# Batch 1's first Fourier step moved into the first items, with the data as stationary operand

## The chip, the cores and the metric

The kernel runs on 1 core of one Trainium2 chip. The metric is the device time of one execution in microseconds (us), the median of several runs. TensorE (PE) multiplies matrices; PEld is its weight load; VectorE (DVE), ScalarE (ACT) and GpSimd (POOL) work beside it; SyncE (SP) issues most transfers, in order, and waits at a transfer that may not start yet. Each engine executes its instructions in the order in which they are written.

## The reference

```python
# x: (2, 3008, 256); then an MLP pair on the 6016 rows
X = np.fft.rfft(x, axis=1)
Yr = Xr @ w_r - Xi @ w_i + b_r
Yi = Xr @ w_i + Xi @ w_r + b_i
Yr = np.sign(Yr) * np.maximum(np.abs(Yr) - 0.01, 0.0)     # Yi the same
y = np.fft.irfft(Y, n=3008, axis=1)
h = y @ w_in;  g = np.maximum(h, 0) + alpha * np.minimum(h, 0);  x = g @ w_out
h = x @ w_in2; g = np.where(h >= 1, h, np.where(h <= -1, 0, (h + 1) ** 2 / 4)); return g @ w_out2
```

## The kernel before

The length 3008 is split as 47 x 64. A forward transform is two matmul steps: the **first step** over the 47 (`f1`), the **second step** over the 64 with the twiddle factors (`f2_parts`). Rows of `x` come in 16 groups `g`, 8 for each batch. `f1(g)` has the 96 x 96 matrix of cosines and sines as stationary operand and 4 x 256 columns of x as moving operand; ACT and DVE copy the result from PSUM to a tile `ae`. The second step needs other rows on a partition, so `store_a` writes `ae` to HBM (`a_dr`), in two halves, and `load_a` reads it back as `a_sb[b]`, in parts. All of this is issued on SP in program order, between loads of `x`, `c_f2` (tiles `m`) and `c_i1` (tiles `n`). All 16 groups of `f1` stand ahead of the first item.

Then come 24 **items** (b, i), 12 for each batch, in a loop over `j`. In pass j TensorE executes, in this order: the second step of item j+2 (`psf`, 4 matmuls), a mixing sum of item j+1 (`psk`), two mixing products of item j (`ri`), the inverse transform's first step of item j-2 (`psi`); in passes 16 to 21 also one `p3` (`ps`, 32 matmuls of 64 x 64 tiles), the inverse transform's last step for batch 0. ACT and DVE split `psf` into a high and a low part (`fh`, `fl`) and a sum `s`, add the bias (`ri<-psk,b_t`), shrink, and copy `psi` (`ve`) and `ps` (`yt`). Between the items the weights of the MLP are converted (`conv`). After the loop the MLP begins (`first`: `psh`), a dense run of matmuls to the end.

An fp32 matmul is two instructions in the profile, so 32 matmuls are x64 there.

PSUM has 8 banks. Six belong to tags of one or two buffers in the pool `psum` (`e` has two; `o0` to `o3`, `ri` and `psk` among them, one each); tag `h` has two. A tile that takes a buffer over waits until the last tile in it has been read.

Of the kernel before, what the change touches and what calls it, by code (L numbers as in the profile page):

```python
# [18 lines left out]
NK = 24  # L19
# [12 lines left out]
def fourier_constants():  # L32

    import numpy as np

    n1, k1 = np.arange(R1), np.arange(NK)
    a = 2 * np.pi * (np.outer(n1, k1) % R1) / R1

    c = np.zeros((2, 48, 2, 2, NK))
    for par in range(2):  # L40
        c[par, :R1, 0, par] = np.cos(a)
        c[par, :R1, 1, par] = -np.sin(a)
    c = c.reshape(96, 4, 2, NK // 2).transpose(0, 2, 1, 3).reshape(96, 96)

    g = np.zeros((2, 64, 64))
# [26 lines left out]
    return (c.astype(f), m.reshape(128, NK * 128).astype(f),  # L72
            w.reshape(128, NK * 128).astype(f), g.astype(f))
# [21 lines left out]
def spectral_mlp_kernel(ctx: ExitStack, tc: tile.TileContext, x, w_r, w_i, bias, c_f1, c_f2,  # L95
                        c_i1, c_i2, w_in1, w_out1, alpha, w_in2, w_out2, out):
# [5 lines left out]
    psum = ctx.enter_context(tc.tile_pool(name="psum", bufs=2, space=PSUM))  # L102
    dram = ctx.enter_context(tc.tile_pool(name="dram", bufs=1, space=DRAM))
# [29 lines left out]
    a_dr = [[dram.tile([NT, 48, D], F32, name=f"a_dr{b}_{h}") for h in range(2)] for b in range(B)]  # L133
# [214 lines left out]

    c47 = block("u2", [128, 1024], F32, "c47")[0:96, 0:96]
    A.dma_start(c47, c_f1)  # L350
    xs = {}

    def load_x(g):
        b, j = divmod(g, 8)
        tag = f"p{g}" if g < 6 else f"w{g - 6}" if g < 14 else f"c{g - 12}"
        xs[g] = block(tag, [96, 4, D], F32, f"x{b}_{j}")
        if g == 0:
            nc.sync.dma_start(xs[g][:, 0:1, :], x[b, j, :, 0:1, :])
            nc.sync.dma_start(xs[g][:, 1:4, :], x[b, j, :, 1:4, :])
        else:  # L360
            nc.sync.dma_start(xs[g], x[b, j])
# [3 lines left out]
    def load_a(b, parts):  # L365
        if a_sb[b] is None:
            a_sb[b] = block(f"a{b}", [128, NK, D], F32, f"a_{b}")
        for k, n in parts:
            h, k0 = divmod(k, NK // 2)
            src = a_dr[b][h].rearrange("t (q k) f -> (t q) k f", q=4)  # L370
            nc.sync.dma_start(a_sb[b][:, k:k + n, :], src[:, k0:k0 + n, :])

    def store_a(g, h):
        b, j = divmod(g, 8)
        nc.sync.dma_start(a_dr[b][h][4 * j:4 * j + 4].rearrange("t p f -> p t f"), aes[g][48 * h:48 * h + 48])
# [7 lines left out]
    a_sb, aes = [None] * B, {}  # L383

    def f1(g):
        b, j = divmod(g, 8)
        if g < 10:
            ae = block(f"w{8 + g}" if g < 5 else f"m{1 + g}" if g < 8 else f"w{g - 8}", [96, 4, D], F32, f"ae{g}")
        else:
            if g == 10:  # L390
                late.append(block("a1", [96, 6, 4, D], F32, "ae_late"))
            ae = late[0][:, g - 10]
        aes[g] = ae
        for i in range(2):
            ps = psum.tile([96, 2, D], F32, tag="h" if i else "e", name=f"ps1_{b}_{j}_{i}")
            for u in range(2):
                T.matmul(ps[:, u, :], c47, xs[g][:, 2 * i + u, :], start=True, stop=True)
# [5 lines left out]
    late = []  # L403
# [5 lines left out]
    slopes = base.tile([128, 128], F32, name="slopes")  # L409
    alpha_t, sign, slope, flips = (slopes[:, NF * k:NF * k + NF] for k in range(4))  # L410
    flips = flips.bitcast(U32)
    A.dma_start(alpha_t, alpha)
# [4 lines left out]
    V.memset(ones, 1.0)  # L417
    for g in range(8):
        f1(g)
        store_a(g, 0)  # L420
        load_x(8 + g)
        if g == 3:
            load_mn(0, m_t, c_f2, 0)
        if g in (1, 2):
            A.dma_start(wm32[g - 1], (w_r, w_i)[g - 1].rearrange("(c p) e -> p c e", p=128))
    load_a(0, A_PARTS[:2])
    load_mn(0, m_t, c_f2, 1)
    load_a(0, A_PARTS[2:5])
    load_mn(1, m_t, c_f2, 0)
    load_mn(0, n_t, c_i1, 0)  # L430
    for g in range(8):
        store_a(g, 1)
    load_mn(1, m_t, c_f2, 1)
    load_mn(0, n_t, c_i1, 1)
    load_a(0, A_PARTS[5:])
# [3 lines left out]
    next(conv)  # L439
# [3 lines left out]
    def f2_parts(b, i, **where):  # L443

        ps = psum.tile([128, 2, 2, 2, R2], F32, **(where or {"tag": "h"}), name=f"psf{b}_{i}")
        for k in range(2):
            for c in range(2):
                T.matmul(ps[:, :, c, k, :], a_sb[b][:, 2 * i + k, c * 128:(c + 1) * 128],
                         m_t[i // 4][:, (2 * i + k) % 8, :], start=True, stop=True)
        return lambda: parts_of(b, i, ps)  # L450

    def parts_of(b, i, ps):
# [3 lines left out]
        ps = ps.rearrange("p t c k n -> p (t c k n)")  # L456
        t = rot.tile([128, 512], F32, tag="ta" if (b, i) < (0, 2) else "tb", name=f"s32_{b}_{i}")
        xi, s32 = t[:, 0:256], t[:, 256:512]
        xt[b, i] = tuple(v.rearrange("p (t c n) -> p t c n", t=3, c=2) for v in (xh, xl))

        def op(name):
            if name == "i":
                A.activation(xi, ps[:, 256:512], AF.Copy)
            elif name == "s":
                V.tensor_tensor(s32, ps[:, 0:256], xi, op=ALU.add)
            elif name == "H":
                A.activation(xh[:, 0:512], ps, AF.Copy)
            elif name == "L":
                V.tensor_tensor(xl[:, 0:512], ps, xh[:, 0:512].bitcast(F32), op=ALU.subtract)
            elif name == "h":  # L470
                A.activation(xh[:, 512:768], s32, AF.Copy)
            elif name == "l":
                V.tensor_tensor(xl[:, 512:768], s32, xh[:, 512:768].bitcast(F32), op=ALU.subtract)
# [14 lines left out]

    wm = [block(t, [128, 2, 2, D], F32R, f"wm{k}") for k, t in enumerate(("c0", "c1", "w2"))]
    ws = [rot.tile([128, 2, D], F32, tag=t, name=f"ws{t}") for t in ("cm", "cp")]  # L490

    def split_wm(k, w):
        hi, lo = (wm[k][:, z].rearrange("p c (h q) -> p c q h", h=2) for z in range(2))
        split(w.rearrange("p c (q h) -> p c q h", h=2), hi, lo, A)

    for g in range(8, 16):
        f1(g)
        if g < 15:
            store_a(g, 0)
        if g == 8:  # L500
            T.matmul(ri[0].rearrange("p z e -> p (z e)"), ones, b_t[0:1].rearrange("p z e -> p (z e)"), start=True, stop=True)
            V.tensor_copy(b_t, ri[0])
        if g == 9:
            split_wm(0, wm32[0])
            V.scalar_tensor_tensor(ws[0], wm32[0], -1.0, wm32[1], op0=ALU.mult, op1=ALU.subtract)
        if g == 11:
            split_wm(1, ws[0])
            V.tensor_tensor(ws[1], wm32[1], wm32[0], op=ALU.subtract)
        if g == 13:
            split_wm(2, ws[1])  # L510
# [118 lines left out]
    def first(l, c, f, before):  # L629
        n = chunks[c][2]  # L630
        xh, xl = xc[l, c]
        tag = "e" if f % 2 and (c > 4 or c < 2 and f < 4 - 2 * c) else "h"
        ps = psum.tile([128, NMAX], F32, tag=tag, name=f"psh{l}_{c}_{f}")[:, :n]
# [36 lines left out]
    ops = [f2_parts(*items[0], tag="o3", bufs=1), f2_parts(*items[1], tag="e"), None]  # L670
    ops[:2] = [v() for v in ops[:2]]
    for what in "0i 0s 0h 1i 0l 0H 1s 0L 1h k0 1l 1H f2 r0 1L 2i".split():
# [6 lines left out]
        else:  # L679
            ops[int(what[0])](what[1])  # L680
    for name in "HshLl":
        ops[2](name)
    store_a(15, 0)
    for j in range(n):
        parts = f2_parts(*items[j + 2]) if 0 < j < n - 2 else None
        if j + 1 < n:
            mix_sum(*items[j + 1])
        if parts is not None:
# [5 lines left out]
        if j == 3:  # L694
            for g in range(8, 16):
                store_a(g, 1)
        if j == 5:
            load_a(1, A_PARTS[:2])
        if j == 6:
            load_mn(2, n_t, c_i1, 0)  # L700
            load_a(1, A_PARTS[2:3])
            load_mn(2, n_t, c_i1, 1)
            load_a(1, A_PARTS[3:5])
        if j == 9:
            load_a(1, A_PARTS[5:])
# [19 lines left out]
    prep(0, 1)  # L725
    first(0, 0, 0, None)
# [174 lines left out]
    def quad(p, j, prev, extra, last=False):  # L901
# [5 lines left out]
        def product_of(op):  # L907
            if op in ("M1", "M5"):
                k = "AC"[op == "M5"]
                ps[k] = psum.tile([128, NMAX], F32, tag="h", name=f"ps{k}{l}_{p}_{j}")[:, :m]  # L910
# [177 lines left out]
```

## Time and profile before

| | |
|---|---|
| median of 3 runs | 1102.14 us (1100.82 to 1102.43) |
| profiled execution | 1102.65 us, of which its span 1100.6 us |
| PE busy | 1087.2 us (99%) |
| DVE, ACT, POOL busy | 897.4, 815.9, 36.9 us |
| DMA | 101.19 MB, mean 92 GB/s |

The span is the time from the first to the last instruction. A busy share is that of an engine over the whole span; the kernel has stages, so what a change of one stage is worth is read from the rows of that stage. A row of the timeline merges neighbours that are alike; its bracket says how long the engine was idle before it and what ended that.

### The profile page before, as it was taken

The page shows a single profiled execution, that of the slowest core. Times are in us where ns is not written, and L with a number is a line of the kernel's source. Part 1 is how long each engine was busy: PE and PEld are TensorE (multiplying, and loading weights), DVE is VectorE, ACT ScalarE, POOL GpSimd, SP SyncE. Part 2 cuts the span into 40 slices and gives each one's busy share as a digit, 9 for nine tenths or more (in the row PEclk, how much of TensorE's full clock was granted, in tenths as well). Part 3 has the DMA queues.
Part 4 walks back from the last instruction along what each step waited for, and adds up shares of the span by engine and source line. Part 5 has one row for each costly group of instructions (what it writes and reads, how often), then busy time and mean ns, then how long its engine had stood idle before and what let it go on. Part 6 is the DMA issues. An engine that isn't in the chain of part 4 may idle for free.

```text
span 1100.6 us, 17043 instructions
## 1 busy us (share of the span) xinstructions
PE 1087.2 (99%) x6368; PEld 955.7 (87%) x6368; DVE 897.4 (82%) x1572; ACT 815.9 (74%) x1499; POOL 36.9 (3%) x36
## 2 busy tenths in 40 slices
PE   9989999999999999999999999999999999999998
PEld 6878888888888998888889988888899888888897
DVE  3769759888879979989999877877878878878876
ACT  3557776656776768888888777877778878777876
POOL 0025400000000000000000000000000000000000
PEclk9999999999999999999999999999999999999999
DMA  9898754101322403324226720010010000100101
GB/s 265 299 277 261 204 142 108 39 1 67 126 97 97 171 20 115 115 96 141 89 97 248 273 90 1 1 39 1 1 38 1 37 1 1 39 1 1 39 1 37
DMA packets 49860, 101.19 MB, mean 92 GB/s; under 512 B 5009, under 2 KB 27249, under 8 KB 49778
## 3 DMA queue, kind: packets, MB, share of 16 engines
q1 hardware_dynamic: 48832, 99.41, 27.6%
q8 instruction: 50, 0.82, 0.3%
q10 hardware_dynamic: 946, 0.69, 0.2%
q14 instruction: 32, 0.26, 0.1%
HBM read 64.57 MB, written 35.52 MB: 91 GB/s over the span
## 4 chain that ended last, share of the span: by engine, by line
PE 82%; ACT 3%; DVE 2%; issue 0%; ACTq 0%; DVEq 0%
PE pq L114 10%; PE pq L115 10%; PE pq L116 10%; PE seeded L114 4%; PE seeded L116 4%; PE seeded L115 4%; PE psh L114 4%; PE pso L114 4%; PE psh L116 4%; PE psh L115 4%; PE pso L116 4%; PE pso L115 4%; PE psA L114 3%; PE psA L116 3%; PE psA L115 3%; PE psC L116 3%
## 5 line engine op out<-in xcount | busy, mean ns | idle before, releaser
L114 PE MATMUL pq<-gh,w 128*128 128x512 f32 (+1 forms) x576 | 216.6, 376 | 1.0 <-ACT yt L874 1.0
L115 PE MATMUL pq<-gl,w 128*128 128x512 f32 (+1 forms) x576 | 216.0, 375 | 0.4 <-DVE gl L845 0.2
L116 PE MATMUL pq<-gh,w 128*128 128x512 f32 (+1 forms) x576 | 215.8, 375 | 0.0
L842 ACT ACTIVATE gh<-ta 128x512 fp32r<-128x512 f32 (+1 forms) x144 | 88.0, 619 | 92.1 <-DVE ta L839 85.9
L641 ACT ACTIVATE ta<-psh,slopes 128x512 f32<-128x512 f32 (+1 forms) x96 | 65.1, 678 | 78.7 <-DVE ta L643 42.3
L114 PEld LDWEIGHTS pq<-gh,w 128*128 128x128 f32 x576 | 108.8, 189 | 15.9 <-ACT yt L874 3.1
L115 PEld LDWEIGHTS pq<-gl,w 128*128 128x128 f32 x576 | 108.9, 189 | 13.7 <-DVE gl L845 1.0
L116 PEld LDWEIGHTS pq<-gh,w 128*128 128x128 f32 x576 | 108.9, 189 | 12.8
L845 DVE TENSOR_TENSOR gl<-tb,gh 128x512 fp32r<-128x512 f32 (+1 forms) x96 | 65.3, 680 | 60.8 <-ACT gh L842 60.7
L845 DVE TENSOR_TENSOR gl<-ta,gh 128x512 fp32r<-128x512 f32 (+1 forms) x144 | 97.3, 676 | 3.1 <-ACT gh L842 1.4
L111 DVE TENSOR_TENSOR gl<-ta,gh 128x512 fp32r<-128x512 f32 (+1 forms) x96 | 65.2, 679 | 37.9 <-ACT gh L108 37.5
L933 DVE TENSOR_TENSOR h<-psC,s 128x512 f32<-128x512 f32 (+1 forms) x72 | 48.8, 678 | 40.8 <-PE psC L116 34.1
L114 PE MATMUL psh<-mxh,w 128*128 128x512 f32 (+1 forms) x192 | 72.2, 376 | 0.1
L114 PE MATMUL pso<-gh,w 128*128 128x512 f32 (+1 forms) x192 | 72.3, 377 | 0.0
L116 PE MATMUL pso<-gh,w 128*128 128x512 f32 (+1 forms) x192 | 71.9, 375 | 0.0
L115 PE MATMUL psh<-mxl,w 128*128 128x512 f32 (+1 forms) x192 | 71.9, 375 | 0.0
L116 PE MATMUL psh<-mxh,w 128*128 128x512 f32 (+1 forms) x192 | 71.9, 375 | 0.0
L115 PE MATMUL pso<-gl,w 128*128 128x512 f32 (+1 forms) x192 | 71.9, 375 | 0.0
L643 DVE SCALAR_TENSOR_TENSOR ta<-psh,slopes,ta 128x512 f32<-128x512 f32 (+1 forms) x96 | 70.5, 734 | 0.0
L839 DVE SCALAR_TENSOR_TENSOR tb<-tb,h 128x512 f32<-128x512 f32 (+1 forms) x96 | 60.7, 673 | 0.0
L831 ACT ACTIVATE ta<-ta 128x512 f32<-128x512 f32 (+1 forms) x96 | 59.3, 617 | 1.6
L842 ACT ACTIVATE gh<-tb 128x512 fp32r<-128x512 f32 (+1 forms) x96 | 59.3, 618 | 0.0
(163 smaller groups left out, 2640.1 us busy)
## 6 DMA issues: line engine op xcount, KB each, us to landing
s<-kept SPq DMA_DIRECT2D x32, 512.0 KB, 4.3
u<-in_w_in SPq DMA_DIRECT2D x32, 256.0 KB, 3.0
u<-in_w_out SPq DMA_DIRECT2D x32, 256.0 KB, 3.3
kept<-sh SPq DMA_DIRECT2D x16, 512.0 KB, 2.9
kept<-wh SPq DMA_DIRECT2D x16, 512.0 KB, 2.7
w<-kept SPq DMA_DIRECT2D x16, 512.0 KB, 5.5
v_dr<-ve SPq DMA_DIRECT2D x12, 512.0 KB, 3.9
v<-v_dr SPq DMA_DIRECT2D x32, 192.0 KB, 5.3
```

The source lines that it names most:

```text
L111: V.tensor_tensor(lo, src, hi.bitcast(F32), op=ALU.subtract)
L114: T.matmul(ps, wl, xh, start=start, stop=False, skip_group_check=chained)
L115: T.matmul(ps, wh, xl, start=False, stop=False, skip_group_check=chained)
L116: T.matmul(ps, wh, xh, start=False, stop=stop, skip_group_check=chained)
L641: A.activation(ta, ps, AF.Copy, scale=slope[:, f:f + 1])
L643: V.scalar_tensor_tensor(ta, ps, sign[:, f:f + 1], ta, op0=ALU.mult, op1=ALU.max)
L831: A.activation(self.t, self.t, AF.Square)
L839: V.scalar_tensor_tensor(self.t, self.t, 1.0, self.h, op0=ALU.min, op1=ALU.max)
L842: A.activation(halves(self.gh, self.m), like_halves(self.t, self.m), AF.Copy)
L845: V.tensor_tensor(halves(self.gl, self.m), like_halves(self.t, self.m), halves(self.gh, self.m).bitcast(F32), op=ALU.subtract)
L933: V.tensor_tensor(blk.h, ps[x], ps[y_], op=ALU.add)
```

## The change

Batch 0 keeps its first step, its stores and its loads. For batch 1 `f1` is replaced by `f1_points(g)`: x is the stationary operand, 64 of its columns at a time on 64 (or 48) partitions, and 48 columns of cosines and sines (`c_p1`, held in `slopes[:, 64:128]`) are the moving operand. Its 32 matmuls for a group go to four 64 x 64 tiles of the array. The result has the layout that the second step wants, so two copies put it into `a_sb[1]`, and nothing goes to HBM. Groups 8 and 9 stand ahead of the first item, groups 10 to 15 in passes 0 to 5, between `psk` and `ri`. The second step of batch 1 is now 8 matmuls of 64 rows for an item, with its own constants (`c_p2`, tiles `mp`, 6 loads of 512 KB); its result takes two banks, so tag `h` becomes a pool of its own that holds two buffers of one bank, then, from pass 10 to the end of the loop, one buffer of two banks. The inverse step's `psi` moves to tag `e` from pass 10 on. Loads of batch 1's x move behind the first loads of `a_0`, and the splits of the mixing weights (`split_wm`) and the bias matmul move into and behind batch 0's `f1`.

```diff
-    for g in range(8, 16):
-        f1(g)
-        if g < 15:
-            store_a(g, 0)
...
+    def f1_points(g, second=V):
+
+        v = xs[g].rearrange("p (q d n) -> p q d n", q=2, d=8)
+        ps = [psum.tile([128, 8, 2 * NK], F32, tag="e", name=f"ps1_1_{g}_{r}") for r in range(2)]
+        for d in range(8):
+            for q in range(2):
+                for r, rows in enumerate((slice(0, 64), slice(64, 112))):
+                    T.matmul(ps[r][64 * q:64 * q + 64, d, :], v[rows, q, d, :], g47[rows, 0:48], start=True, stop=True)
+
+        def evict():
+            for r in range(2):
+                d0 = 16 * (g - 8) + 8 * r
+                dst, src = a_sb[1][:, :, d0:d0 + 8], ps[r].rearrange("p d k -> p k d")
+                if r and second is V:
+                    V.tensor_copy(dst, src)
+                else:
+                    A.activation(dst, src, AF.Copy)
...
+            ps = htile([128, 2, 2, 2, 2, R2], name)[:, :, 0]
+            for k in range(2):
+                n = 2 * i + k
+                for z in range(2):
+                    for c in range(2):
+                        rows = slice(64 * c, 64 * c + 64)
+                        T.matmul(ps[:, c, :, k, :], a_sb[1][rows, 2 * n + z, :], mp_t[n // 4][rows, n % 4, z, :],
+                                 start=z == 0, stop=z == 1)
...
-        ps = [psum.tile([128, D], F32, tag="h", name=f"psi{b}_{i}_0"),
+        ps = [htile([128, D], name) if (b, i) < (0, 8) else psum.tile([128, D], F32, tag="e", name=name),
...
+    f1_points(8)()
+    late = f1_points(9)
...
     for j in range(n):
+        if j == 10:
+            h_pool(1)
         parts = f2_parts(*items[j + 2]) if 0 < j < n - 2 else None
         if j + 1 < n:
             mix_sum(*items[j + 1])
+        if j < 6:
+            late = f1_points(10 + j, A)
...
-        if j == 3:
-            for g in range(8, 16):
-                store_a(g, 1)
-        if j == 5:
-            load_a(1, A_PARTS[:2])
+        if j < 6:
+            late()
+        if j in (5, 7, 8, 9, 11, 12):
+            load_mp((5, 7, 8, 9, 11, 12).index(j))
```

The order of instructions changes at three places that matter below. The first is TensorE in pass 0, around the mixing products of item 0. Before:

```order
L486 MATMUL psk_1_379<-wm_239,fl_1_342 128x256 [waits DVE_49]
L486 MATMUL psk_1_379<-wm_239,fl_1_342 128x256
L486 MATMUL ri_77<-wm_240,fh_0_338 128x256 x4
L486 MATMUL ri_77<-wm_240,fl_0_339 128x256 x2
L486 MATMUL ri_77<-wm_241,fh_0_338 128x256 x4
```

After (`ps_1_10` is group 10 of the first step; 30 more of its matmuls follow where the dots are):

```order
L566 MATMUL psk_1_384<-wm_128,fl_1_346 128x256 [waits DVE_49]
L566 MATMUL psk_1_384<-wm_128,fl_1_346 128x256
L440 MATMUL ps_1_10_0_392<-slopes,x_105 64x48 [waits DVE_49,DMAHW6_49,PE_49,Pool_49]
L440 MATMUL ps_1_10_1_393<-slopes,x_105 64x48 [waits DVE_49]
...
L566 MATMUL ri_75<-wm_129,fh_0_337 128x256 x4
```

Group 10 now stands ahead of the products, and its second matmul waits for DVE: its buffer of tag `e` is that of `psk_1`, which DVE reads in `ri_76<-psk_1`. On DVE that instruction now has a copy more ahead of it, four rows up:

```order
L549 TENSOR_TENSOR fl_1_346<-psf_1_340,fh_1_345 128x512 [waits Activation_49]
L447 COPY a_92<-ps_1_9_1_299 128x48x8
L545 TENSOR_TENSOR s_0_2_373<-psf_2_366,s_0_2_373 128x256 [waits PE_49,Activation_49]
L549 TENSOR_TENSOR fl_2_372<-psf_2_366,fh_2_371 128x512 [waits DMAHW3_49]
L553 TENSOR_TENSOR fl_2_372<-s_0_2_373,fh_2_371 128x256 [waits Activation_49]
L575 TENSOR_TENSOR ri_76<-psk_1_384,b_t 128x512 [waits PE_49]
```

Without that copy (and with other numbers) DVE's rows here are those of before. The third place is TensorE in pass 16, where `psi` is followed by the first `p3`. Before:

```order
L544 MATMUL psi_2_0_1266<-y_1_2_1152,n_103 128x256
L544 MATMUL psi_2_1_1267<-y_1_2_1152,n_103 128x256
L613 MATMUL ps_0_0_0_1276<-slopes,v_0_1098 64x47 [waits DMAHW2_49,DMAHW1_49]
L613 MATMUL ps_0_0_1_1277<-slopes,v_0_1098 64x47 [waits DMAHW2_49]
L613 MATMUL ps_0_0_0_1276<-slopes,v_0_1098 64x47
```

After:

```order
L602 MATMUL psi_2_0_1517<-y_1_2_1395,n_123 128x256
L602 MATMUL psi_2_1_1518<-y_1_2_1395,n_123 128x256
L671 MATMUL ps_0_0_0_1527<-slopes,v_0_1337 64x47 [waits DMAHW5_49,DMAHW0_49]
L671 MATMUL ps_0_0_1_1528<-slopes,v_0_1337 64x47 [waits DMAHW1_49,Activation_49]
L671 MATMUL ps_0_0_0_1527<-slopes,v_0_1337 64x47
```

The second matmul of `p3` now waits for ACT too: three tiles in turn (`psi_2_0` and the two of `p3`) share the two buffers of tag `e`, so the second tile of `p3` takes the buffer of the `psi` just ahead of it, which ACT has yet to copy.

## Rows read from the trace of the kernel before

**Rows 1.** The page: span, and each engine's busy time.
```profile
span 1100.6 us, 17043 instructions
PE 1087.2 (99%) x6368; PEld 955.7 (87%) x6368; DVE 897.4 (82%) x1572; ACT 815.9 (74%) x1499; POOL 36.9 (3%) x36
```

**Rows 2.** Waits of PE, whole span: total us, times, longest us.
```profile
PE psf L448 <- ACT fh L471: 1.7, 1, 1.7
PE psf L448 <- DVE fl L469: 1.3, 1, 1.3
PE pq L114 <- ACT yt L874: 1.0, 1, 1.0
PE psi L544 <- ACT ve L548: 1.0, 2, 0.7
```

**Rows 3.** Timeline of PE: start, us, line, operands, count, idle before.
```profile
5.03 16.29 PE L397 MATMUL ps<-x,c 96*96 96x256 f32 x72
...
35.19 1.16 PE L448 MATMUL psf<-m,a 128*128 128x128 f32 x8
36.54 1.13 PE L448 MATMUL psf<-m,a 128*128 128x128 f32 x8 [0.19 <-DMA a<-a_dr]
...
40.75 0.61 PE L486 MATMUL ri<-wm,fh 128*128 128x256 f32 x4
...
152.33 0.48 PE L114 MATMUL psh<-mxh,w 128*128 128x512 f32 x1
```

**Rows 4.** Timeline of SP: the last store of the first half, the first loads.
```profile
25.34 0.32 SPq L375 DMA_DIRECT2D a_dr<-ae  x1
...
31.98 2.02 SPq L371 DMA_DIRECT2D a<-a_dr  x2
```

**Rows 5.** DMA issues, 25.3 to 25.7 us: KB, us from issue to landing.
```profile
a_dr<-ae SPq DMA_DIRECT2D x1, 192.0 KB, 6.5
```

**Rows 6.** Windows: busy us (x) by engine, PE clock, DMA share, GB/s.
```profile
22.00:26.00 4.00, 4.00 (x18) 2.85 (x18) 2.36 (x4) 2.18 (x3) 0.00 (x0) 1.00 1.01 309
```

**Rows 7.** Timeline of DVE: the bias addition of item 1.
```profile
42.52 0.69 DVE L518 TENSOR_TENSOR ri<-psk,b_t 128x512 f32<-128x512 f32 x1
```

**Rows 8.** Timeline of PE, pass 16: psi, p3, psf.
```profile
110.65 1.14 PE L544 MATMUL psi<-y,n 64*128 64x256 f32 x8
111.71 1.15 PE L613 MATMUL ps<-slopes,v 48*64 48x47 f32 x64
112.79 1.16 PE L448 MATMUL psf<-m,a 128*128 128x128 f32 x8
```

**Rows 9.** Timeline of PE, passes 0 to 3: products, psi, psf, psk.
```profile
41.20 0.39 PE L486 MATMUL ri<-wm,fl 128*128 128x256 f32 x2
41.42 0.61 PE L486 MATMUL ri<-wm,fh 128*128 128x256 f32 x4
...
47.87 0.39 PE L486 MATMUL ri<-wm,fl 128*128 128x256 f32 x2
48.19 1.13 PE L544 MATMUL psi<-y,n 64*128 64x256 f32 x8
49.25 1.16 PE L448 MATMUL psf<-m,a 128*128 128x128 f32 x8
50.17 0.69 PE L486 MATMUL psk<-wm,fh 128*128 128x256 f32 x4
```

**Rows 10.** Timeline of ACT: copies of psi and p3, and two waits.
```profile
69.33 0.66 ACT L548 ACTIVATE ve<-psi 128x256 f32<-128x256 f32 x2 [3.35 <-DMA v_dr<-ve]
...
80.02 0.67 ACT L163 ACTIVATE cm<-u 128x512 f32<-128x512 f32 x1 [2.62 <-DMA u<-in_w_out]
...
111.81 0.66 ACT L548 ACTIVATE ve<-psi 128x256 f32<-128x256 f32 x2 [0.19 <-PE psi L544]
112.91 0.86 ACT L617 ACTIVATE yt<-ps 128x376 f32<-128x376 f32 x2 [0.44 <-PE ps L613]
```

**Rows 11.** Timeline of PE, 5 to 6 us: the first matmuls on x.
```profile
5.03 1.40 PE L397 MATMUL ps<-x,c 96*96 96x256 f32 x3
```

More of the change, by code (lines that the diff above doesn't have):

```diff
@@ L363, in spectral_mlp_kernel @@
-    A_PARTS = ((0, 2), (2, 2), (4, 2), (6, 2), (8, 4), (12, 6), (18, 6))
[L365 to L375, printed above, removed]
@@ L377, in load_mn @@
-    def load_mn(k, tiles, src, h=None):
-        s = slice(0, 8) if h is None else slice(4 * h, 4 * h + 4)
-        nc.sync.dma_start(tiles[k][:, s, :].rearrange("p k f -> p (k f)"),
-                          src[:, 1024 * k + 128 * s.start:1024 * k + 128 * s.stop])
[L383 to L397, printed above, removed]
-            if i == 0:
-                A.activation(ae[:, 0:2, :], ps, AF.Copy)
-            else:
-                V.tensor_copy(ae[:, 2:4, :], ps)
@@ L403, in spectral_mlp_kernel @@
-    late = []
-    for g in range(8):
-        load_x(g)
-    m_t = [block(f"m{k}", [128, 8, 128], F32, f"m{k}") for k in range(3)]
-    n_t = [block(f"m{3 + k}", [128, 8, 128], F32, f"n{k}") for k in range(3)]
-    wm32 = [rot.tile([128, 2, D], F32, tag="tb", name=f"wm32_{k}") for k in range(2)]
     slopes = base.tile([128, 128], F32, name="slopes")
@@ new lines, in spectral_mlp_kernel @@
+    for g in range(13):
+        new_x(g)
+    for g in range(8):
+        load_x(g)
+    m_t = [block(f"m{k}", [128, 8, 128], F32, f"m{k}") for k in range(3)]
+    n_t = [block(f"m{3 + k}", [128, 8, 128], F32, f"n{k}") for k in range(3)]
+    wm32 = [rot.tile([128, 2, D], F32, tag="tb", name=f"wm32_{k}") for k in range(2)]
+    wm = [block(t, [128, 2, 2, D], F32R, f"wm{k}") for k, t in enumerate(("c0", "c1", "w2"))]
+    ws = [rot.tile([128, 2, D], F32, tag=t, name=f"ws{t}") for t in ("cm", "cp")]
@@ L432, in spectral_mlp_kernel @@
         store_a(g, 1)
+    for g in range(13, 16):
+        new_x(g)
+    load_x(12)
+    load_mn(0, n_t, c_i1, 1)
     load_mn(1, m_t, c_f2, 1)
-    load_mn(0, n_t, c_i1, 1)
-    load_a(0, A_PARTS[5:])
+    load_x(13)
+    load_a(A_PARTS[5:6])
+    load_x(14)
+    load_a(A_PARTS[6:])
+    load_x(15)
     load_mn(1, n_t, c_i1)
@@ L443, in f2_parts @@
     def f2_parts(b, i, **where):
[L445 to L449, printed above, removed]
+        name = f"psf{b}_{i}"
+        if b == 0:
+            shape = [128, 2, 2, 2, R2]
+            ps = psum.tile(shape, F32, name=name, **where) if where else htile(shape, name)
+            for k in range(2):
+                for c in range(2):
+                    T.matmul(ps[:, :, c, k, :], a_sb[0][:, 2 * i + k, c * 128:(c + 1) * 128],
+                             m_t[i // 4][:, (2 * i + k) % 8, :], start=True, stop=True)
+            ps = ps.rearrange("p t c k n -> p t c (k n)")
+        else:
+            ps = htile([128, 2, 2, 2, 2, R2], name)[:, :, 0]
+            for k in range(2):
+                n = 2 * i + k
+                for z in range(2):
+                    for c in range(2):
+                        rows = slice(64 * c, 64 * c + 64)
+                        T.matmul(ps[:, c, :, k, :], a_sb[1][rows, 2 * n + z, :], mp_t[n // 4][rows, n % 4, z, :],
+                                 start=z == 0, stop=z == 1)
+            ps = ps.rearrange("p c t k n -> p t c (k n)")
         return lambda: parts_of(b, i, ps)
```

173 lines of the change are left out of this document (111 added, 62 removed).

## The prediction

> **What bounds the kernel now.** I read the page first: PE is busy for 1087.2 of the 1100.6 us of the span [rows 1], so the time is that of TensorE's chain, and the other engines matter only where TensorE waits for them. The view of waits says where it does: the longest ones are 1.7, 1.3, 1.0 and 0.7 us, and only the third (`pq`) belongs to the MLP; the others are in the items [rows 2]. The reader is to see that nothing behind the items has slack: if the MLP's run begins earlier or later, the end moves by the same amount. So I follow TensorE by its timeline: the first step of both batches from 5.03 us, 72 instructions in 16.29 us (0.226 us each); the second step of item 0 at 35.19; the products of item 0 at 40.75; the MLP's second `psh` group at 152.33, from where the run is dense [rows 3]. The whole question is how far 152.33 moves. For the start I read SP's timeline, the landing of one store and the rate of the transfers [rows 4 to 6].
>
> **The start (term a).** What the change removes is 64 of the 128 instructions of `f1`, 14.5 us at 0.226 us [rows 3]. It doesn't move item 0 by that much, since that work hid batch 0's way through memory. The last store of batch 0's first half is issued at 25.34 and lands 6.5 us later, at 31.8 [rows 4, 5]; the first load of `a` follows at 31.98 and TensorE uses it at 35.19, the second load at 36.54, for which it waits 0.19 [rows 3, 4]. So transfers are only just hidden now, and will not be when TensorE is done with batch 0 at about 20.6 (5.03 + 64 x 0.226 + the bias matmul). How early the store lands is a matter of what the queue carries ahead of it. Before, that was 15 loads of x; after, it is 10, and one more half of `m`: 5 x 384 KB less and 256 KB more, 1.7 MB, or 5.5 us at 309 GB/s [rows 6]. The store lands at 26.3, the load 3.2 us later, at 29.5; I take 29.2, as no load of x is on its way in front of it any more. Term a is -6.0 us. Bounds: 28.2 if the x load ahead cost its whole 1.3 us (384 KB at 309 GB/s), and 30.9 if the load takes the 4.6 us that the second one took (31.98 to 36.54): -7.0 to -4.3. Groups 8 and 9 of the new first step lie in TensorE's gap between 20.6 and 29.2 and cost nothing; if the gap were gone, they would cost 2.4 us (below).
>
> **Pass 0 (term b).** Group 10 stands between `psk` of item 1 and the products of item 0, and waits until DVE has added the bias to that `psk`, because it takes over its bank. That addition ended at 42.52 + 0.69 = 43.2, 8.0 us behind the start of item 0's second step [rows 3, 7]; it stands on DVE behind the splits of item 2, and one new copy of 384 columns more is ahead of it (about 0.4, as two such copies of ACT take 0.86 [rows 10]), part of which fits into a gap. So group 10 starts 8.2 us after item 0, where the products now start 5.56 after it [rows 3]: +2.6 us. Behind it are queued the products, and all the rest. Bounds: 0 if DVE comes to the addition at once, 2.9 if the new copy counts in full.
>
> **Six groups inside the items (term c).** The shape is that of `p3`: 32 matmuls of 64 x 64 tiles on 47 columns, 64 instructions that stand 1.08 us apart from what follows [rows 8], 17 ns for each. In front of them TensorE goes from the whole array to tiles. That shows in the rows: two `ri` matmuls take 0.22 us when `ri` follows (41.20 to 41.42), 0.32 when `psi`, which uses half arrays, follows (47.87 to 48.19) [rows 9]: 0.10 for a switch. Six groups cost 6 x 1.18 = +7.1 us, all on the path, as TensorE has no idle time in passes 0 to 5. Bounds: 6.5 without the switch, 7.7 with a second one in each. Their copies on ACT take 0.9 us of a pass that grows by 1.2 and end about when the next group needs the banks (ACT copies `psi` 1.16 us after its start for 0.66 [rows 8, 10], then these; the next group starts 2.7 after it), so I cost them at nothing; if they were 0.5 us later it would be 5 x 0.5.
>
> The Trainium skill speaks against such a swap (TensorEngine Tiling (Array Packing), Instruction Overhead): a matmul has an overhead of some 60 cycles, so a dimension that is already small shouldn't be made the moving one. By it, 64 instructions at 25 ns (60 cycles at 2.4 GHz, an estimate from that page) would be 1.6 us for a group and 9.6 for six, 2.5 more than in my sum. The trace has 17 ns each for the same shape, since four tiles work side by side; the row decides.
>
> **The second step of batch 1 (term d).** An item has 16 instructions of 64 rows and 128 columns instead of 8 of 128 rows. No row shows that shape. The nearest is `psi`: 8 of 64 rows and 256 columns, so as many columns on each half of the array, and its halves overlap: 1.06 us (48.19 to 49.25), where the second step now takes 0.92 (49.25 to 50.17) [rows 9]. I take +0.14 for each of 12 items: +1.7 us. Bounds: 0, and, if the halves worked one after the other, 16 x 0.115 = 1.84 us for an item, +11.
>
> **Banks (terms e and f).** In pass 10 the second step takes both banks of tag `h`, one of which holds the `psi` just ahead. ACT starts to copy a `psi` 1.16 us after its first matmul (110.65, 111.81) and needs 0.66 for both halves, some 0.38 for the first [rows 8, 10]; TensorE goes on 1.06 after it. It waits 0.5 to 0.6 us, once: +0.6 (term e). The same happens in each of passes 16 to 21: the second matmul of `p3` takes the bank of that `psi`. `p3` began at 111.71, the copy ends at about 112.2: 0.55 each, six times, +3.3 us (term f). Bounds: 0, and 4.6 if it must wait for both halves (112.47).
>
> **Waits that go (term g).** The 16 stores and the loads of batch 1's `a` leave SP's queue. Behind the stores stood the store of `ve`, for which ACT waited 3.35 us, and behind a load that waits for them stood a load of weights, 2.62 us [rows 10]. TensorE's waits of 1.7, 1.3 and 0.7 [rows 2] follow from these: -3.7 us. Of the new transfers, `mp` is 3 MB in passes 5 to 12, as much as the loads of `a` were. Bound: 0, if `mp` and the late loads of x delay the same stores.
>
> **The sum.** -6.0 + 2.6 + 7.1 + 1.7 + 0.6 + 3.3 - 3.7 = +5.6 us. The profiled execution took 1102.65 and becomes 1108.2; it is 0.5 above the median of the runs shown, so the forecast is 1107.7.
>
> **The rivals.**
> *Bank waits not paid* (the other side). The order shows which instruction waits for which, not for how long. If ACT and DVE are done with the banks in pass 0, pass 10 and passes 16 to 21 when TensorE comes, terms b, e and f fall away, 6.5 us: 1101.2. For it: ACT and DVE have slack there (74% and 82% busy [rows 1]). Against it: rows 7 and 8 give the ends of these very copies, later than TensorE's next start. From 3.4 us not paid on, the kernel isn't slower.
> *A shorter way through memory.* If the first load lands before 25.8, the sum falls below +2.2, and the result is no change: about 1104. Against it: the queue is at its full share around there (1.01) [rows 6].
> *TensorE starts slowly after its gap.* It has 2.4 us of work between 20.6 and 29. The granted clock is 1.00 (2.4 GHz) where I read it [rows 6], but the first three matmuls on x, after an idle start, took 1.40 us, 0.43 apart, twice the later pace [rows 3, 11]. If item 0 to 2 start at that pace, their 4.7 us of TensorE work up to 40.75 take up to 4.7 more; I take 2, as DVE's chain of term b covers part: 1109.7. The Trainium skill has this as a rule (TensorE: Matmul & The Clock Gate, HAM oscillation — how this bites in real kernels): after idle time TensorE goes back to 1.2 GHz. The trace of before shows no fall behind a gap, and its longest wait is 1.7 us [rows 2].
> *Halves one after the other* (term d's upper bound): +9.3, 1117. Against it: `psi` and `p3` overlap.
>
> **How the numbers follow.** The forecast has 0.50 (own range 1105.5 to 1109.7), bank waits not paid 0.17, a shorter way 0.15, the slow start 0.12, serial halves 0.06. A measurement of this kernel tells a change from none at about 0.2%, 2.2 us: below 1099.9 is faster, above 1104.3 slower. Of the 0.17, 0.09 is faster (the smaller c or d with it) and 0.08 the same; of the 0.15, 0.03 faster, 0.08 the same, 0.04 slower. So faster 0.12, same 0.16, slower 0.72. The range of 1101.5 to 1110.5 leaves out the serial halves and the lower half of the first rival.
>
> **What would show it.** After: `psf` of item 0 between 28 and 31 us, with TensorE idle ahead of it, ended by a transfer (a); a wait of PE on DVE's `ri<-psk` of 2 to 3 us (b); 32 matmuls of group 10 to 15 in 1.1 to 1.2 us (c); `psf` of batch 1 in 1.06 us (d); six waits of `p3` for `ve`, 0.5 us each (f); no wait of 1 us or more between passes 6 and 9 (g). I'd be wrong most by term d, whose shape no row has, by a late x in passes 2 to 5, or if the items turn out to wait for ACT.

## The result, and the profile after

The changed kernel takes 1117.37 us (median of 4 runs, 1115.96 to 1118.84) where the kernel before takes 1102.29 beside it: 1.0135 times as long, 95% interval 1.0111 to 1.0159. It is slower, as forecast, but by 15.1 us and not 5.6; the forecast of 1107.7 and its range up to 1110.5 miss it. The profiled span is 1116.4 us, 15.8 more than in [rows 1].

The page: the span, TensorE's busy time, and the queue that brings instructions (packets, MB, share).

```profile
span 1116.4 us, 18109 instructions
PE 1093.5 (98%) x6912; PEld 963.4 (86%) x6912; DVE 892.3 (80%) x1566; ACT 816.9 (73%) x1505; POOL 44.3 (4%) x44
q8 instruction: 54, 0.88, 0.3%
```

Waits of PE (total us, times, longest us), to be held against [rows 2]:

```profile
PE ps L440 <- DMA x<-in_x: 4.7, 1, 4.7
PE psi L602 <- issue: 2.6, 1, 2.6
PE ps L440 <- issue: 2.4, 2, 1.8
PE ps L440 <- DVE ri L575: 1.4, 1, 1.4
PE ps L671 <- ACT ve L606: 1.4, 6, 0.2
...
PE psk L566 <- ACT a L449: 0.9, 1, 0.9
...
PE psf L518 <- ACT fh L551: 0.6, 1, 0.6
PE psf L528 <- ACT ve L606: 0.5, 1, 0.5
```

The waits of 1.7 and 1.3 us of [rows 2] are gone (0.6 is left). New are the wait for x, the two waits for a bank in pass 0 (1.4 and 0.9), and 5.0 us of "issue", in which TensorE waits for nothing that the profile names. Of these, 0.63 us stand ahead of group 9; in e1 and e11 below, the same 0.63 us are put down to ACT's copy of group 8. The theory is about the other two, 4.4 us. The timeline of PE shows where (columns as in [rows 3]):

```profile
26.11 1.96 PE L440 MATMUL ps<-slopes,x 64*64 64x48 f32 x64 [4.66 <-DMA x<-in_x]
28.70 2.02 PE L440 MATMUL ps<-slopes,x 64*64 64x48 f32 x64 [0.63 <-issue]
30.64 3.78 PE L518 MATMUL psf<-m,a 128*128 128x128 f32 x16
...
37.15 0.71 PE L566 MATMUL psk<-wm,fh 128*128 128x256 f32 x4 [0.91 <-ACT a L449]
...
39.98 1.14 PE L440 MATMUL ps<-slopes,x 48*64 48x48 f32 x62 [1.39 <-DVE ri L575]
41.05 0.73 PE L566 MATMUL ri<-wm,fh 128*128 128x256 f32 x4
...
43.29 1.89 PE L518 MATMUL psf<-m,a 128*128 128x128 f32 x8
...
49.96 1.04 PE L440 MATMUL ps<-slopes,x 64*64 64x48 f32 x55
52.76 0.37 PE L440 MATMUL ps<-slopes,x 48*64 48x48 f32 x9 [1.77 <-issue]
...
60.03 1.13 PE L602 MATMUL psi<-y,n 64*128 64x256 f32 x6
63.81 0.59 PE L602 MATMUL psi<-y,n 64*128 64x256 f32 x2 [2.65 <-issue]
...
168.68 0.48 PE L134 MATMUL psh<-mxh,w 128*128 128x512 f32 x1
```

The reader is to see three things. The MLP's second `psh` stands at 168.68, 16.35 later than in [rows 3], so the loss is all in the items. Group 12 stops after 55 of its 64 instructions, and `psi` of pass 3 after 6 of 8, where no semaphore is waited for. And groups 8 and 9 take 1.96 and 2.02 us each, nearly twice group 10's 1.14. The windows give the clock (columns of [rows 6]):

```profile
24.50:34.80 10.30, 8.06 (x147) 7.87 (x148) 3.53 (x6) 2.73 (x6) 0.00 (x0) 0.50 0.75 218
34.80:41.60 6.80, 4.27 (x87) 3.74 (x87) 4.98 (x10) 3.11 (x8) 0.20 (x1) 1.00 1.05 344
41.60:45.00 3.40, 3.40 (x19) 3.40 (x17) 0.77 (x2) 1.36 (x3) 0.74 (x1) 0.50 1.05 322
45.00:65.50 20.50, 16.08 (x289) 14.04 (x289) 8.51 (x18) 9.09 (x22) 0.00 (x0) 1.00 0.94 255
65.50:68.90 3.40, 3.40 (x72) 3.08 (x72) 1.95 (x4) 1.38 (x4) 0.00 (x0) 0.50 0.48 160
```

TensorE's clock is at 1.2 GHz (0.50) in three stretches, 17 us in all: behind its gap for x, behind the waits of pass 0, and behind the second stall. Before it was 1.00 throughout the items.

**The theory.** TensorE's instructions come in blocks by a transfer of their own, the 54 packets of 16 KB above; 54 x 256 is 13,824, its 6912 matmuls and 6912 weight loads. The new groups use up 128 instructions in 1.1 us, and where the transfers are full a block comes too late. The Trainium skill states the blocks (Runtime: NRT & Kernel Launch, Instruction fetch mechanics: refills in blocks of 256 instructions, fetched ahead on a queue of the engine's own), and that crossing a boundary is "mostly hidden"; the two stalls say that here it is not. Rivals: the stalls belong to the data or to those instructions; or the fall of the clock, not the stalls, is the cost.

### The profile page after: what moved, and what is told of

The parts are those of the page before. It is cut to its first block, busy times and chain, and to the rows that moved or that the text cites. A ratio compares the mean times of both kernels' runs of the same rounds, so it can differ in the third digit from the quotient of the medians.

```text
span 1116.4 us, 18109 instructions
## 1 busy us (share of the span) xinstructions
PE 1093.5 (98%) x6912; PEld 963.4 (86%) x6912; DVE 892.3 (80%) x1566; ACT 816.9 (73%) x1505; POOL 44.3 (4%) x44
## 4 chain that ended last, share of the span: by engine, by line
PE 81%; ACT 3%; DVE 2%; issue 0%; ACTq 0%; DVEq 0%
PE pq L134 10%; PE pq L135 10%; PE pq L136 10%; PE seeded L134 4%; PE seeded L135 4%; PE seeded L136 4%; PE psh L134 4%; PE pso L134 4%; PE psh L135 4%; PE psh L136 4%; PE pso L135 3%; PE pso L136 3%; PE psA L134 3%; PE psA L136 3%; PE psA L135 3%; PE psC L136 3%
```

## The experiments

**e1: keep TensorE busy in its gap.**

```diff
+    for _ in range(5):
+        T.matmul(ri[1].rearrange("p z e -> p (z e)"), warm[:, 0:128], warm, start=True, stop=True)
     f1_points(8)()
```

> Five matmuls of 512 columns on zeros stand in TensorE's gap ahead of group 8 (21.4 to 26.1 us in the changed kernel); they add work and change no result. Theory (TensorE's clock fell in that gap, and the fall costs time): the granted clock stays at 1.00 to 36 us, groups 8 and 9 take 1.1 us each instead of 1.96 and 2.02, the second step of items 0 and 1 takes 1.9 instead of 3.8, and the MLP's second psh comes 2 to 4 us earlier than 168.68. Rival (the chain through ACT and DVE sets the items' start anyway): the matmuls are faster, but the MLP moves by less than 0.7 us. A second question of this run: two stalls stand inside groups of instructions with no semaphore, ahead of TensorE's instructions number 961 and 1218 (counted in its own stream, weight loads included). If they are the engine's wait for its next block of 256 instructions, they stay at 961 and 1218 (give or take one), and so move 20 instructions earlier in the program, which has 20 more ahead of it; if they belong to the data or the place in the program, they stay at the same matmuls (981 and 1238).

Measured: 1113.85 us (1.0104, 1.0074 to 1.0134). The timeline of PE:

```profile
25.92 1.15 PE L440 MATMUL ps<-slopes,x 64*64 64x48 f32 x64 [0.22 <-DMA x<-in_x]
...
30.82 3.37 PE L518 MATMUL psf<-m,a 128*128 128x128 f32 x16 [1.46 <-DMA a<-a_dr]
...
40.81 0.71 PE L566 MATMUL ri<-wm,fh 128*128 128x256 f32 x4
```

Groups 8 and 9 run at full pace, but the second step now waits for `a` and starts no earlier, so up to there the rival holds: until the second step starts, that fall of the clock cost nothing. Behind that wait the clock fell again (0.51 from 31.2 to 34.6), so what half pace costs in items 0 and 1 is not separated; `ri` comes 0.24 earlier. The second `psh` comes 6.8 earlier because neither stall shows in this execution:

```profile
161.86 0.48 PE L134 MATMUL psh<-mxh,w 128*128 128x512 f32 x1
```

Its four runs lie at 1111.5, 1111.6 (the profiled one), 1116.1 and 1117.3, so the median says little of the clock. The question on the stalls' place stays open here.

**e2: group 10 behind the products.**

```diff
-        if j < 6:
+        if 0 < j < 6:
             late = f1_points(10 + j, A)
...
         mix(*items[j])
+        if j == 0:
+            late = f1_points(10, A)
```

> Group 10 moves behind the mixing products of item 0 in pass 0; nothing else moves. Theory (term b: the products are queued behind group 10, which waits for DVE's bias addition): the waits of 1.4 and 0.2 us go, ri of item 0 starts at about 38.4 instead of 41.05, group 10 follows at about 40.2 without a wait, and the MLP's second psh comes 1.6 us earlier than 168.68, up to 3 if the clock doesn't fall a second time at 41.6. Rival (DVE and ACT set the pace of passes 0 and 1 anyway): the wait shows again at psf or psk of pass 1, and the MLP moves by less than 0.5 us.

Measured: 1111.50 us (1.0081, 1.0049 to 1.0113). The waits of 1.4 and 0.2 went but for 0.27, the products follow `psk` at once, and the clock didn't fall a second time:

```profile
35.65 0.39 PE L566 MATMUL psk<-wm,fl 128*128 128x256 f32 x2
35.88 0.61 PE L566 MATMUL ri<-wm,fh 128*128 128x256 f32 x4
...
37.89 1.14 PE L440 MATMUL ps<-slopes,x 48*64 48x48 f32 x62 [0.27 <-DVE ri L575]
```

Term b is confirmed: from item 0's second step to that of item 3 it takes 10.03 us (28.93 to 38.96) instead of 12.65 (30.64 to 43.29). The whole gain, 9.4 us at `psh` (159.24), is not its price: in this execution x came 2 us earlier and no stall shows, but group 12 waits 2.02 us for x.

**e3: fewer transfers.** Groups 12 to 15 compute on other groups' x.

```diff
-        v = xs[g].rearrange("p (q d n) -> p q d n", q=2, d=8)
+        v = xs[g if g < 12 else 10 + g % 2].rearrange("p (q d n) -> p q d n", q=2, d=8)
...
-    load_x(12)
```

> Leaves out the loads of x for groups 12 to 15 (4 x 384 KB, asked for between 41 and 47 us); these groups compute on the x of groups 10 and 11, so batch 1's output is of other data. All instructions of TensorE stay. Theory (the stalls of 1.77 us inside group 12 and 2.65 us inside psi of pass 3 are instruction blocks that come late through transfer queues that are full until 62 us): the blocks that start at 49.99 and 61.43 start some 2 to 5 us earlier relative to TensorE's place in its stream, both stalls fall below 0.4 us, the clock doesn't fall at 65.5, and the MLP's second psh comes 4 to 6.5 us earlier than 168.68. Rival (the stalls belong to those instructions or to a wait that the profile doesn't name): they stay, and the MLP moves by less than 1 us.

Measured: 1111.72 us (1.0082, 1.0062 to 1.0102). Both stalls are gone, the clock doesn't fall at 65.5, and the second `psh` stands at 162.95, 5.7 earlier. One profile without a stall says little, since those of e1 and e2 have none either. But all four runs took 1110.1 to 1113.1 us, where the four of the changed kernel took 1116.0 to 1118.8, and the transfers of both blocks begin further ahead of need (the table under e9). So the stalls depend on how much is being transferred.

**e4: p3 ahead of the products.**

```diff
             parts_now(parts())
+        if 16 <= j < 22:
+            p3(j - 16)
         mix(*items[j])
```

> In passes 16 to 21 p3 (and its two copies on ACT) moves from behind psi to ahead of the products ri, so that it no longer takes a bank of the psi just ahead of it. Theory (term f: p3 waits 0.5 us for ACT's copy of psi in each pass): passes 16 to 21 are 5.3 to 5.5 us long instead of 5.97, and the MLP's second psh comes 3 to 4 us earlier than 168.68. Rival (psi then waits for ACT's copies of p3, which share its bank, or ACT falls behind with fh): the passes stay at 5.8 to 6.2 us, and the MLP moves by less than 1 us.

Measured: 1115.87 us (1.0118, 1.0097 to 1.0139). A pass takes 5.44 us (137.22 to 142.66) instead of 5.97, and `p3` no longer waits:

```profile
137.22 1.06 PE L528 MATMUL psf<-mp,a 64*128 64x128 f32 x16
...
139.08 1.15 PE L671 MATMUL ps<-slopes,v 48*64 48x47 f32 x64
...
142.66 1.06 PE L528 MATMUL psf<-mp,a 64*128 64x128 f32 x16
```

Term f holds, with some 3 us. At `psh` only 1.7 are left (166.95), because the stalls were there again, ahead of the same instructions, and `psf` of pass 15 stood 1.1 later than in the changed kernel.

**e5: n1 and m2 loaded later.**

```diff
-    load_mn(1, n_t, c_i1)
-    load_mn(2, m_t, c_f2)
...
+        if j == 3:
+            load_mn(1, n_t, c_i1)
+            load_mn(2, m_t, c_f2)
```

> The loads of n1 and m2 (512 KB each; first used in pass 6) move from ahead of the loop into pass 3; the computation is whole, and TensorE's instructions and their order are those of the changed kernel. Theory (the stalls at TensorE's instructions 961 and 1218 are instruction blocks that stand behind the data transfers of 36 to 62 us): 1 MB, 3.3 us at 309 GB/s, leaves the full stretch, the two blocks start ahead of 49.99 and 61.43, both stalls shrink below 0.5 us in the profile, its third fall of the clock (65.5) goes, and the median falls by 3 to 6 us, to 1111 to 1114. Rival (the stalls come from which engine the block's packet lands on, or other chance, and not from how much is queued): stalls of 1.5 us or more stay at 961 or 1218, and the median moves by less than 1.5 us.

Measured: 1116.23 us (1.0108, 1.0088 to 1.0129). The second stall is gone, the first is longer (2.62 us), and the third fall of the clock didn't go but comes earlier, behind that stall (0.50 from 53.9 to 57.3 us). So it is mostly a miss: ahead of the first block (50.25) stand x 13 to 15 and parts of `a`, asked for from 42.49 to 45.97 us, and the loads of u moved up to 46.60 from 49.85 into the place of n1 and m2. Taking 1 MB out of the order doesn't thin the queue where others follow at once; e3, which takes the bytes away, does.

**e8 and e9: move the boundaries.** e8 differs from what its expectation says: its second loads of x stand ahead of group 8 in the program, which therefore waits 36 us, and its 48 columns lie in the bank in which `ri` adds up, so it doesn't compute the same (e9 has them elsewhere).

```diff
+    load_x(8)
+    load_x(9)
...
+    for _ in range(32):
+        T.matmul(ri[1][0:64, 0, 0:48], warm[0:64, 0:64], warm[0:64, 0:48], start=True, stop=True)
     f1_points(8)()
```

> Two edits to the changed kernel: 32 matmuls of 48 columns on zeros, which are 128 instructions of TensorE with their weight loads, in its gap ahead of group 8, where it is idle; and the x of groups 8 and 9 is loaded a second time behind x 15 (768 KB more, for nothing), so that the transfers stay full longer. Results don't change. Theory (a block of 256 instructions that comes late): the stalls stay at TensorE's instructions 961 and 1218 of its own stream, give or take one, so they now stand inside psf of item 4 in pass 2 (with 5 of its 8 matmuls begun) and inside group 13 in pass 3 (with 18 or 19 of its 64 begun); group 12 and psi of pass 3 run through. Rival (they belong to the data or the place in the program): they stay inside group 12 and psi of pass 3, at 1089 and 1346 of the stream.

Measured: 1145.92 us, no stall, so neither is told apart. It shows something else: its items run when the transfers have ended (DMA share 0.24 from 64 to 72 us, 0.01 from 72 to 80), and from item 0's second step to the second `psh` they take 130.65 us (65.18 to 195.83), where the changed kernel takes 138.04 with the same instructions. Nearly all of the 7.4 us lies in passes 2 to 4. They are not the price of full transfers as such: e1's profile has full transfers (DMA share 1.03 from 48 to 56 us) without a stall of 0.5 us or more, and takes 131.04 us (30.82 to 161.86). They are the price of the stalls and of the half pace behind the second.

```diff
+    idle = psum.tile([64, 48], F32, tag="o2", bufs=1, name="idle")
+    for _ in range(8):
+        T.matmul(idle, warm[0:64, 0:64], warm[0:64, 0:48], start=True, stop=True)
     f1_points(8)()
```

> Eight matmuls of 48 columns on zeros, 32 instructions of TensorE with their weight loads, in its gap ahead of group 8, into a bank that is overwritten later; nothing else is changed. Theory (a block of 256 instructions that comes late): where TensorE stalls between 46 and 66 us, it does so ahead of instruction 961 or 1218 of its own stream (give or take one), which now is ahead of the 40th matmul of group 12 (not the 56th) and some 16 matmuls ahead of the 7th psi of pass 3, in its ri or in group 13. Rival (the data, or the place in the program): the stalls stay ahead of the 56th matmul of group 12 and the 7th psi of pass 3, at 993 and 1250. If no stall shows in this execution, the run tells nothing on this.

Measured: one run, 1113.52 us. Both stalls are there, and both moved by 32 instructions:

```profile
49.15 0.80 PE L440 MATMUL ps<-slopes,x 64*64 64x48 f32 x39
50.47 0.60 PE L440 MATMUL ps<-slopes,x 48*64 48x48 f32 x25 [0.52 <-issue]
...
56.44 0.49 PE L566 MATMUL ri<-wm,fh 128*128 128x256 f32 x2
58.74 0.38 PE L566 MATMUL ri<-wm,fh 128*128 128x256 f32 x2 [1.82 <-issue]
```

Group 12 stops after 39 matmul instructions instead of 55 (16, which are 32 with their weight loads), and the second stall is in `ri`, not `psi`. In TensorE's stream they stand ahead of 961 and 1218 as ever. In this execution the rival is out. The records of the transfers, with the place that TensorE had reached in its stream when the block's transfer began (worked out from the trace; a block later by one is 256 further):

```
kernel   block     transfer, us     TensorE at   stops ahead of, goes on at
before   961       60.20 to 61.07      699       -
before   1217      79.70 to 80.58      985       -
changed  961       49.99 to 51.35      859       961, 52.76
changed  1218      61.43 to 62.58     1217       1218, 63.81
e4       961       50.43 to 51.59      925       961, 53.13
e4       1218      62.25 to 63.42     1210       1218, 64.82
e5       961       50.25 to 51.33      961       961, 52.88
e5       1218      60.11 to 61.21     1180       -
e9       961       47.53 to 48.89      856       961, 50.47
e9       1218      55.99 to 57.40     1170       1218, 58.74
e1       961       47.08 to 48.34      825       -
e1       1218      54.94 to 56.24     1071       -
e2       961       42.60 to 43.48      809       -
e2       1218      52.49 to 53.60     1050       -
e6       961       43.67 to 44.55      796       -
e6       1218      53.48 to 54.71     1084       -
e3       961       46.95 to 47.87      684       -
e3       1218      55.87 to 56.87     1042       -
e8       961       75.41 to 76.83      728       -
e8       1218      81.75 to 82.71      941       -
```

TensorE goes on 1.2 to 1.6 us after the block's transfer ends. In the kernel before the transfers began 230 to 260 instructions ahead of need, which then were 15 to 18 us of work; in e8, whose transfers had ended, 230 to 280 ahead. Under full transfers the changed kernel and e1, e2, e4, e5, e6 and e9 have anything from 0 to some 170, with a stall mostly where it is little. In e1 the second block came just too late: four matmul instructions of `ri` take 0.83 us instead of 0.61, and TensorE goes on at 57.46, 1.2 behind the transfer. What decides when a transfer begins is not shown.

**e6: three moves together** (the edits of e2, e4 and e5).

> Three moves together: group 10 behind ri in pass 0, p3 ahead of ri in passes 16 to 21, the loads of n1 and m2 in pass 3. Theory (the three costs add): 1117.4 less 2 to 3 for the first, 2.8 for the second, 3 to 6 for the third: 1105.5 to 1109.5, still slower than the kernel before, since the six groups of 1.1 us and the wait for batch 0's way through memory stay. Rival (the first and the third save the same wait for transfers): 1110 to 1113.

Measured: 1106.29 us (1.0030, 1.0013 to 1.0046). That is inside the forecast, and the rival is out. Beside the kernel before, the changed kernel loses 15.1 us, e2 9.0, e4 13.3, e5 12.5 and e6 2.6: alone the three moves gain 6.1, 1.8 and 2.6 us, 10.5 in all, together 12.5. So their costs add, and something more is saved: e4 alone still had both stalls in its profile and e5 one. Which of the moves keeps them away is not shown, and one of the ten runs took 1113.49. `psh` stands at 156.75, 4.4 later than before, without a stall:

```profile
30.73 3.48 PE L516 MATMUL psf<-m,a 128*128 128x128 f32 x16
...
156.75 0.48 PE L134 MATMUL psh<-mxh,w 128*128 128x512 f32 x1
```

**e10 and e11: x earlier, with and without filling the gaps.** To e6 they add (e10 has the six matmuls on zeros besides, written as in e1):

```diff
+    load_x(10)
+    load_x(11)
     load_a(A_PARTS[:3])
-    load_x(10)
...
+    load_x(12)
     for g in range(8):
         store_a(g, 1)
...
-    late = f1_points(9)
+    f1_points(9)()
```

> The three moves of e6, and: x 10 and 11 are loaded ahead of the first loads of a (not between them), x 12 ahead of the stores of the second half; the copies of group 9 stand right behind it; and six matmuls on zeros, five ahead of group 8 and one behind group 9, keep TensorE busy. Theory: the waits of 0.9 us for the copy of group 9 and 0.9 us for x go; with the clock at 1.00 the second step of items 0 and 1 takes 1.9 us instead of 3.5 and items start 0.5 to 1 us earlier; the MLP's second psh at 153.5 to 155 (156.75 in e6), the median 1103 to 1105. Rival (x 10 and 11 hold up the loads of a by up to 2.5 us, 768 KB at 309 GB/s): second step of item 0 at 32 to 33 us instead of 30.7, and no gain over e6.

> As e10_early_x_fill, without the six matmuls on zeros. Theory (the fall of the clock costs at the items' start, since the matmuls there stand on the chain with ACT and DVE): 0.5 to 1 us slower than e10, with the clock at 0.50 from 24 to 34 us and the second step of items 0 and 1 in 3.5 us. Rival (the landing of a sets the start, as in e1): the same time as e10 within 0.4 us at the MLP's second psh.

Measured: 1106.69 (1.0028, 1.0014 to 1.0041) and 1107.14 us (1.0042, 1.0024 to 1.0059), no gain over e6. The waits for group 9's copy and for x 12 went, but the rival holds: the loads of x hold up those of `a`, and the second step starts at 33.28 and 32.29, the second `psh` at 158.07 and 157.10. So e11, without the filling, is not slower in the profile, and its median lies within the noise of e10's. e10's filling ended ahead of its last wait, 3.07 us for `a`, and its second step ran at half pace too (3.32 us); so nothing is learned of the clock's price.

**e7 and e12: the waits that term g removes, in the kernel before.** e7 has the edit of e5. e12 changes SP's order alone:

```diff
-        if g < 15:
+        if g < 10:
             store_a(g, 0)
...
         if j == 3:
+            for g in range(10, 16):
+                store_a(g, 0)
             for g in range(8, 16):
...
-        if j == 5:
-            load_a(1, A_PARTS[:2])
...
             next(conv)
+        if j in (5, 6, 9):
+            load_a(1, A_PARTS[:2] if j == 5 else A_PARTS[2:5] if j == 6 else A_PARTS[5:])
```

> The kernel before with the one move of e5: the loads of n1 and m2 in pass 3. Theory (the transfers of 36 to 62 us hold up the stores of ve and the weights, from which TensorE's waits of 1.7, 1.3 and 0.7 us in passes 6 to 9 follow): these waits shrink by 1 to 3 us in all, and the median is 1099 to 1101.5. Rival (n1 and m2 come too late for pass 6, or the stores of batch 1 behind them do): no gain or up to 2 us more, with a wait of psf or psi for a transfer.

> The kernel before, with only SP's order changed: six of batch 1's first-half stores move behind the store of ve in pass 3, and in passes 5, 6 and 9 the loads of a move behind the loads of weights. Theory (term g: TensorE's waits of 1.7, 1.3 and 0.7 us in passes 6 to 9 come from the store of ve and a load of weights that stand behind those stores and loads): the waits go, the MLP's second psh comes 2.5 to 3.7 us earlier than 152.33, and the median is 1099 to 1101.5 where that of before is 1102.5 to 1103.7. Rival (the queue carries as much in the same stretch, and the waits are only put off): no gain, within 1 us of before, or a new wait of batch 1's second step for a.

Measured: e7 1108.13 us (1.0044, 1.0029 to 1.0059): the rival, m2 comes too late and `psf` waits 7.8 us for it (the waits of 1.7, 1.3 and 0.7 us are gone). The loss of 4.4 us is more than the 2 that the rival had. e12: 1100.85 us beside 1103.36, ratio 0.9977 (0.9965 to 0.9988): the only version faster than the kernel before. Its second `psh` stands at 150.72, 1.6 earlier, less than expected; waits of 1.5 and 1.3 us for `fh` and `fl` are still there, two passes later, so most of the wait is only put off. Why they come back there was not tried.

## Why the prediction was wrong

The 16.35 us at the second `psh`, stretch by stretch (starts of `psf` in the two timelines), beside the forecast's terms:

| stretch | forecast | measured |
|---|---|---|
| start to item 0's second step (a) | -6.0 | -4.55 |
| to `ri` of item 0 (b and one group of c) | +3.8 | +4.85 |
| to the second step of item 8 (five groups of c) | +5.9 | +14.65 |
| to that of item 18 (part of d, e, g) | -2.2 | -2.9 |
| to the second `psh` (f, the rest of d) | +4.1 | +4.3 |

The starts of `psf` of items 3 and 8 in the kernel before:

```profile
42.09 1.06 PE L448 MATMUL psf<-m,a 128*128 128x128 f32 x8
...
61.74 1.16 PE L448 MATMUL psf<-m,a 128*128 128x128 f32 x8
```

In the changed kernel (item 3 stands at 43.29 above), group 14 and item 8:

```profile
66.58 1.96 PE L440 MATMUL ps<-slopes,x 64*64 64x48 f32 x64
...
76.70 1.16 PE L518 MATMUL psf<-m,a 128*128 128x128 f32 x8
```

In e8, items 3 and 8:

```profile
78.04 1.06 PE L520 MATMUL psf<-m,a 128*128 128x128 f32 x8
...
103.89 1.16 PE L520 MATMUL psf<-m,a 128*128 128x128 f32 x8
```

**The step that failed** is in term c: six groups at 1.18 us "all on the path, as TensorE has no idle time in passes 0 to 5", which counts their time and takes their instructions as there whenever wanted, and TensorE's pace as that of before. The runs showed in its place that TensorE stands still for instruction blocks and runs at half pace there. With the transfers out of the way (e8), the second step of item 8 comes 25.85 us behind that of item 3, 6.2 more than before (19.65): 1.24 for a group, inside the term's bounds (6.5 to 7.7 for six). In the changed kernel it comes 33.41 behind, 7.6 more than in e8. Of these, 1.77 + 2.65 are the stalls for instruction blocks, which e9 and e3 show; some 2.2 are half pace behind 41.6 and 65.5: from item 3 to item 4 it takes 5.01 us where e2 takes 4.28, from item 6 to item 7 6.94 where the next pass takes 5.43 (group 14 takes 1.89 instead of 1.08). The rest, 0.9, lies mostly in the passes of the two stalls. Ahead of that, from `ri` of item 0 (41.05) to item 3's second step (43.29), half pace costs 0.9 more (2.24 us instead of 1.34).

That the fall at 41.6 comes of pass 0's waits is what e2 says (the waits of 1.4 and 0.2 shrink to 0.27, and there is no fall). That the fall at 65.5 comes of the stall is what e3 says (no stall, no fall), and e4 and e5, where the clock falls behind stalls of 2.21, 1.71 and 2.62 us. Not every stall is followed by a fall: those of 1.77 us here and of 1.82 us in e9 are not.

The stalls are not the whole miss. The two runs of e1 at 1111.5 us, about 9 more than the kernel before beside them, lie outside the forecast's range too.

**Term a** was 1.45 too large and within its bounds: `a` isn't there earlier, as e1 shows. The long wait of the gap is for x of group 8 (4.66 us), not for `a` as forecast: the second step follows group 9 without a wait. **Term b** had the mechanism: 1.4 + 0.2 us at group 10 instead of 2.6, and ahead of it a like wait of 0.9 for ACT's copy of group 9 (`psk` takes its bank), which the prediction had not seen: 2.5 together. **Term d** is 0: an item of batch 1 is 4.16 us long as before, and its second step 0.99 (119.63 to 120.62), so serial halves are out. That this rival's 1117 is the time that was measured is chance. **Terms e** (0.5) and **f** hold: `p3` to `psf` takes 1.61 us (123.89 to 125.50) instead of 1.08 [rows 8], as forecast, though the row of waits names only 0.2 of it; 0.2 more a pass went elsewhere. The second step, `p3` and the next `psf`:

```profile
119.63 1.06 PE L528 MATMUL psf<-mp,a 64*128 64x128 f32 x16
120.62 0.71 PE L566 MATMUL psk<-wm,fh 128*128 128x256 f32 x4
...
123.89 0.31 PE L671 MATMUL ps<-slopes,v 48*64 48x47 f32 x2
...
125.50 1.16 PE L528 MATMUL psf<-mp,a 64*128 64x128 f32 x16
```

**Term g** held in size (the waits of 3.7 us became 0.6). Its cause, the stores ahead of `ve`, is not shown: in e12, which moves six of those stores and the loads of `a`, most of the wait comes back later.

**The rivals.** Bank waits were paid. No shorter way through memory. TensorE did start slowly after its gap, which the prediction had at 0.12 and 2 us; what that fall cost in items 0 and 1 is not separated (e1, e10). The falls whose price shows came later, behind waits in the middle of the items, where the prediction had looked for none. The Trainium skill's rule that it cited (TensorE: Matmul & The Clock Gate, HAM oscillation) agrees with these rows.

Open: what decides when a block's transfer begins, and so why the runs of one kernel differ (e1's by 5.7 us, which would fit stalls in the slower two, of which there is no profile); and what half pace in items 0 and 1 costs.

## What to carry to other kernels

Price an instruction not by its time alone: many short matmuls can use up instruction blocks faster than they come when transfers are full, so count instructions per us against the stretch's DMA share, and look for idle time inside a group with no semaphore. Where a change opens a gap on a dense TensorE, ask what it waits for next and whether the clock falls there. And a wait for a bank that takes the place of another is found in the order, word for word; its price was right here.

## What was not expected of the hardware

A full stretch alone doesn't stall TensorE, nor does a fast one: the kernel before ran without a stall at DMA share 1.01 to 1.04 (52 to 60 us) with 35 matmul instructions in 4 us, and passes 16 to 21 of the changed kernel, with 108 in 6 us, at DMA shares of 0.35 to 0.76. Both together stall it in the changed kernel and hardly in e1's profile (0.2 us). In the order before, changed (twice), e1:

```profile
52.00:56.00 4.00, 4.00 (x35) 3.50 (x35) 2.48 (x6) 2.47 (x6) 0.00 (x0) 1.00 1.01 396
142.00:148.00 6.00, 5.77 (x108) 4.95 (x106) 3.13 (x7) 4.30 (x11) 2.38 (x2) 1.00 0.76 210
40.00:64.00 24.00, 19.58 (x359) 17.81 (x360) 9.28 (x20) 9.39 (x22) 0.94 (x1) 0.93 1.01 285
48.00:56.00 8.00, 8.00 (x170) 7.21 (x173) 4.12 (x8) 5.34 (x13) 0.00 (x0) 1.00 1.03 294
```

Sixteen instructions on half the array's rows cost an item no more than eight on all of it (term d).
